# Two sets in one 64x64 stretch of TensorE, separate banks for post-mixes, scaled weights two steps ahead, and the last half tile of the value products in quadrants

## The chip, the cores and the metric

The kernel runs on one core of a Trainium2 chip. A core has TensorE (PE) for matrix products, VectorE (DVE), ScalarE (ACT) and GpSimd (POOL) for element-wise work, and SyncE (SP), whose instruction stream here issues every DMA. Each engine works through its own instructions in the order in which the program gives them, and waits on semaphores for the others. Matrix products are written to PSUM, eight banks of 128 partitions by 512 floats, and are copied from there by ScalarE or VectorE. The metric is the device time of one execution in microseconds (us), the median of several runs.

## What is computed

Eight batches of attention with 12 heads over 448 positions of 64 elements, in which the heads are mixed twice, before the softmax and after it; then a gated network without an activation function.

```python
scores = scale * np.matmul(q, k.transpose(0, 1, 3, 2))
scores = np.einsum('bhij,hg->bgij', scores, w_pre)
scores = scores - np.max(scores, axis=-1, keepdims=True)
attn = np.exp(scores)
attn = attn / (np.sum(attn, axis=-1, keepdims=True) + 1e-09)
attn = np.einsum('bhij,hg->bgij', attn, w_post)
attn_out = np.matmul(attn, v)
x = attn_out.transpose(0, 2, 1, 3).reshape(B * S, H * D)
a = x @ w1
b = x @ w2
h = a * b @ w3
return h @ w_out
```

q, k, v are 8x12x448x64, the mixing matrices 12x12, x is 3584x768, w1 and w2 768x1024, w3 1024x1024, w_out 1024x768.

## The kernel before

**Attention.** A score unit (`qk`, L173 to L187) multiplies two heads' queries and keys for a slice of 64 to 128 rows: four matmuls of 64x64 tiles into two PSUM banks, two ScalarE copies out (L178, L179), and a store to a scratch tensor in HBM (`raw_d`). The rows of scores are then read back in another order (`fetch`, L201): five rows of all 12 heads stand on 60 partitions, and four such halves make a set, two blocks (c) of ten rows. 45 blocks a batch and 8 batches make 180 sets.

Each set m goes through these methods: `mix` multiplies its four 60x448 pieces by the mixing matrix (L219, the sign turned and the scale folded in) into two banks, psm; `largest` takes minima of the negated scores on VectorE (L226); `exp` makes exponentials and their sums on ScalarE (L234); `scale` makes the reciprocals on VectorE (L243, L244) and multiplies the second mixing matrix by them on GpSimd (L246), the scaled weights; `post` multiplies the exponentials by these (L259), 28 small matmuls in the program, into banks 4 and 5, pso, which also transposes the result to keys on partitions; `put` (L273) copies both banks to `mt` on ScalarE. All of these matmuls use TensorE as 64x64 tiles.

When 15 blocks of a batch are there (a third of its rows, called a below), `av` (L300) multiplies them by the values: for each pair of heads, four tiles of keys with 128 keys each, the two heads in the two halves of the array's columns (128x64 tiles). 448 keys are three and a half tiles. The last tile holds the last 64 keys twice, and the half of `mt` that does not belong to a row's half set s is zero, kept zero by a memset of parts of pso at the start. The result of three pairs leaves one bank at once: for the first two batches as a high and a low part (L321, L322), for the others as a copy (L307) that is stored to `x_d`.

**Experts.** The network uses each operand as a high and a low part (128x128 tiles and three products for one). For the first two batches it is computed directly (L521, L552), for the other six in pairs of batches with seven products in place of eight (L701). The low parts are made on GpSimd (L640), the sums of products on VectorE (L655) and ScalarE (L657). Weights come by DMA into buffers, asked for as earlier ones are used up (L392). Before that, in the first 50 steps, w3 and w_out, given as 64-bit words, are converted (`to_f32`, four VectorE instructions a piece, L116 to L120) and multiplied into one matrix (L359); later w1 and w2 are converted as well.

**Order.** The whole order is written out by hand in `run`, as steps n, two for each set. Each engine gets its instructions in just this order. `fetch` of set m+2 stands at even steps, ahead of all other DMAs of that step. At an even step n = 2m VectorE takes the minima of set m, a share of the expert matmuls is issued (`advance`), then come the exponentials of set m, and the rest of the share. At an odd step the division and the scaled weights of set m come first, then half of the share and the other half, then value products (`avs`), the post-mix of set m-1, the pre-mix of set m+1, and score units (`qks`). So each odd step has one stretch of 64x64 work, with full-array work around it. `shares` gives each step so many expert matmuls that all steps are about equally long, with the cost of score units, value products and the rest of a stretch given in numbers of expert matmuls. Lists keep work for later: `ends` (copies out of a bank, flushed at fixed points or when a bank is needed), `soon` (the next step's start) and `later` (mainly DMAs, issued at the next step's start behind `fetch`).

PSUM banks: score units use 0 and 1 (a second one 6 and 7), pre-mixes 2 and 3, post-mixes 4 and 5, value products 0, experts 6 and 7.

## Time and profile before

| | us |
|---|---|
| median of 3 runs | 1456.61 |
| lowest and highest run | 1449.06 and 1458.63 |
| the profiled execution, its own time | 1456.61 |
| its span, from the first to the last instruction | 1454.8 |
| ScalarE's exponentials (L234), busy | 226.6 |
| GpSimd's scaled weights (L246), busy | 180.7 |
| post-mix matmuls (L259), busy | 198.6 |
| value product matmuls (L300), busy | 156.9 |

The page gives for each engine the time in which it had an instruction running. Matmuls overlap, so the sum of their durations says little; what one costs is read from the distance between starts. The program's matmuls on plain floats appear as two instructions each in the trace: the 28 of a post-mix are 56. A row "A x n" in the timeline merges n instructions of one line that follow each other. In rows of groups, the part behind the bar is busy time and mean duration, then how long the engine had been idle just before, and what ended that idle time. In the rows of waits, the numbers are the total, the count and the longest.

### The profile page before, as it was taken

How to read it: one execution, taken by the hardware profiler on the slowest of the kernel's cores; microseconds unless marked ns; L12 is line 12 of the kernel's file. 1: busy time of each engine (PE TensorE's matmuls, PEld its weight loads, DVE VectorE, ACT ScalarE, POOL GpSimd, SP SyncE). 2: the span in 40 equal slices, each digit the busy share in tenths (PEclk: the TensorE clock that was granted, in tenths of full speed). 3: DMA queues.
4: the chain of work that ended last, by engine and by line, in shares of the span. 5: the costliest groups of instructions: out<-in, count | busy, mean ns of one | idle time of the engine just before them, and what ended most of it. 6: DMA issues, size and time to landing. Idle time of an engine off the chain costs nothing.

```text
span 1454.8 us, 45722 instructions
## 1 busy us (share of the span) xinstructions
PE 1390.1 (96%) x18684; PEld 1059.4 (73%) x18684; DVE 739.0 (51%) x1497; ACT 833.1 (57%) x1952; POOL 620.7 (43%) x754
## 2 busy tenths in 40 slices
PE   5789998999999989999999999999999999999998
PEld 2357785776677667776777777777776777899988
DVE  4867565767644544432344445334444447334563
ACT  3876665777756656665555656656655546422231
POOL 1333232444324434632244445444335446446683
PEclk7989998999999999999999999999999999999999
DMA  8998789999999999999989988799879766698875
GB/s 256 365 319 274 237 267 287 311 336 307 316 288 353 348 343 319 368 338 314 311 266 291 319 278 280 234 312 350 288 230 285 236 179 214 206 332 263 240 229 173
DMA packets 203760, 416.86 MB, mean 287 GB/s; under 512 B 20528, under 2 KB 120112, under 8 KB 203472
## 3 DMA queue, kind: packets, MB, share of 16 engines
q1 hardware_dynamic: 203552, 413.94, 87.2%
q8 instruction: 149, 2.44, 0.7%
q14 instruction: 59, 0.48, 0.1%
HBM read 279.77 MB, written 134.09 MB: 284 GB/s over the span
## 4 chain that ended last, share of the span: by engine, by line
PE 78%; DMA 13%; DVE 5%; ACT 3%; issue 1%; SPq 0%; POOL 0%; DVEq 0%; ACTq 0%; POOLq 0%
PE e L701 20%; PE psa L300 10%; PE pso L259 10%; PE psm L219 8%; PE psq L173 7%; PE psf L359 5%; PE eg L521 4%; PE e2o L701 4%; PE e1o L701 4%; PE e3o L701 4%; DMA s_d<-s 3%; PE eo L552 3%; DMA cs<-wo 3%; DMA r<-raw_d 2%; DMA wu<-w_d 2%; ACT e L234 1%
## 5 line engine op out<-in xcount | busy, mean ns | idle before, releaser
L246 POOL TENSOR_SCALAR w<-wpo,ri 128x60 f32<-128x60 f32 x360 | 180.7, 518 | 489.0 <-DVE ri L244 465.8
L226 DVE TENSOR_REDUCE mn<-psm 128x1 f32<-128x448 f32 x360 | 207.8, 619 | 317.0 <-PE psm L219 316.6
L701 PE MATMUL e<-eh,wu 128*128 128x448 f32 x1008 | 297.3, 372 | 6.3 <-DVE c L655 3.2
L273 ACT COPY mt<-pso 128x480 f32<-128x480 f32 x352 | 197.8, 621 | 177.3 <-PE pso L259 177.1
L234 ACT ACTIVATE e<-psm,mn 128x448 f32<-128x448 f32 x360 | 226.6, 642 | 9.6 <-DVE mn L226 9.6
L219 PE MATMUL psm<-r,wsc 60*64 60x448 f32 (+1 forms) x1440 | 197.9, 557 | 32.1 <-ACT e L234 19.9
L701 PEld LDWEIGHTS e<-eh,wu 128*128 128x128 f32 x1008 | 188.0, 188 | 52.5 <-issue 27.4
L259 PEld LDWEIGHTS pso<-w,e 60*64 60x64 f32 x10080 | 174.5, 134 | 50.0 <-issue 44.0
L259 PE MATMUL pso<-w,e 60*64 60x60 f32 x10080 | 198.6, 224 | 0.1
L701 PE MATMUL e<-el,wu 128*128 128x448 f32 x504 | 187.1, 371 | 0.0
L173 PE MATMUL psq<-kq 64*64 64x448 f32 x1176 | 159.5, 546 | 0.6 <-ACT st L178 0.6
L300 PE MATMUL psa<-mt,v 128*64 128x150 f32 (+1 forms) x2304 | 156.9, 293 | 1.9 <-ACT st L178 1.9
L300 PEld LDWEIGHTS psa<-mt,v 128*64 128x64 f32 x2304 | 143.6, 137 | 17.9 <-issue 6.3
L655 DVE TENSOR_TENSOR c<-c,e 128x448 f32<-128x448 f32 x168 | 101.8, 618 | 87.6 <-PE e L701 82.8
L178 ACT COPY st<-psq 128x448 f32<-128x448 f32 x162 | 86.4, 533 | 68.8 <-ACT mt L273 32.8
L521 PE MATMUL eg<-xh,wu 128*128 128x448 f32 x384 | 118.8, 380 | 4.8 <-DMA wu<-w_d 4.8
L640 POOL TENSOR_TENSOR el<-x,eh 128x448 fp32r<-128x448 f32 x90 | 104.2, 1176 | 34.8 <-ACT eh L639 34.8
L701 PEld LDWEIGHTS e<-el,wu 128*128 128x128 f32 x504 | 94.9, 188 | 22.4 <-issue 14.1
L243 DVE TENSOR_SCALAR sa<-sm 128x2 f32<-128x2 f32 x180 | 35.9, 200 | 129.6 <-ACT e L234 129.0
L173 PEld LDWEIGHTS psq<-kq 64*64 64x64 f32 x1176 | 62.2, 136 | 53.8 <-issue 29.8
L521 PEld LDWEIGHTS eg<-xh,wu 128*128 128x128 f32 x384 | 71.8, 190 | 38.1 <-issue 25.3
L179 ACT COPY st<-psq 128x448 f32<-128x448 f32 x162 | 87.7, 541 | 0.0
(99 smaller groups left out, 2011.5 us busy)
## 6 DMA issues: line engine op xcount, KB each, us to landing
r<-raw_d SPq DMA_DIRECT2D x344, 210.0 KB, 4.9
raw_d<-st SPq DMA_DIRECT2D x138, 448.0 KB, 5.4
wu<-w_d SPq DMA_DIRECT2D x104, 384.0 KB, 6.4
wu<-s_d SPq DMA_DIRECT2D x96, 384.0 KB, 4.8
wu<-w_d SPq DMA_DIRECT2D x51, 512.0 KB, 5.6
kq<-kq SPq DMA_DIRECT2D x42, 448.0 KB, 6.2
wu<-s_d SPq DMA_DIRECT2D x36, 512.0 KB, 4.9
x<-x_d SPq DMA_DIRECT2D x72, 224.0 KB, 6.3
```

The source lines that it names most:

```text
L173: nc.tensor.matmul(ps[s][z * PP:(z + 1) * PP], t[rows, q:q + PP], t[rows, k:k + S], start=True, stop=True)
L219: nc.tensor.matmul(ps[s][c * PP:(c + 1) * PP, :S], self.wsc[k], r[k, c], start=True, stop=True)
L226: self.nc.vector.tensor_reduce(mn[:, s:s + 1], self.psm[m][s][:, :S], axis=AX.X, op=ALU.min)
L234: nc.scalar.activation(e, p[:, :S], AF.Exp, bias=mn[:, s:s + 1], scale=-1.0, accum_out=sm[:, s:s + 1])
L246: nc.gpsimd.tensor_scalar_mul(w2[:, s], self.wpo, ri[:, s:s + 1])
L259: nc.tensor.matmul(self.pso[c][z * PP:(z + 1) * PP, at:at + HK], e[k, j * PP:(j + 1) * PP], w2s[k, s], start=True, stop=True)
L273: self.nc.scalar.copy(dst.rearrange("p j g (s i) -> p j s g i", s=2), src)
L300: nc.tensor.matmul(self.psa[rows, g % 3, :W], v[:, j, rows], mt[:, j, 2 * g + s, :W], start=(j == 0), stop=(j == NJ - 1))
L521: nc.tensor.matmul(p, u[:, k % (K1 // 2), x], xs[y][:, k], start=(k == 0 and t == 0), stop=(k == K1 - 1 and t == 2))
L640: nc.gpsimd.tensor_tensor(lo, x, hi.bitcast(F32), op=ALU.subtract)
L655: nc.vector.tensor_tensor(a[out], a[to[0]], p, op=ALU.add)
L701: nc.tensor.matmul(p, w[:, k, x], ops[m, k][y], start=(k == 0 and t == 0), stop=(k == nk - 1 and t == 2))
```

## The change

Steps are grouped by four, for two sets m and m+1 (m even). Step 0 of a group: fetch of both next sets, minima and exponentials of m and m+1. Step 1: divisions and scaled weights of both. Step 3: value products, then post-mix of m, a score unit, post-mix of m+1, pre-mix of m+2, a score unit, pre-mix of m+3, one stretch of 64x64 work. Expert matmuls go to steps 0 to 2. Conversions go on in all steps; at step 3 they come behind the stretch.

The pre-mix and the post-mix of even sets use banks 4 and 5, those of odd sets banks 0 and 1. Score units use banks 2 and 3. One of the two copies of a post-mix is made by VectorE. In `mt` a third's rows are now ordered by half set, then block (s, u, i).

A call of `av` now does two head pairs, in three calls for each third instead of two. The first three key tiles go as before into bank 1; of the last half tile, each half set's columns (75, or 73 at the end of a batch) are multiplied by the 64 keys on their own partitions, into bank 0 for one half set and another part of bank 1 for the other, as four 64x64 tiles. A copy on ScalarE and additions on VectorE join the two and restore the order of rows (`join`). For the first two batches, the high part is then a ScalarE copy and the low part a GpSimd subtraction. In most places the value products come ahead of the post-mix in step 3; for four of the 24 thirds they stand in the steps 0 to 2.

```diff
     def mix(self, m):
-        ps = [self.bank(2 + s, f"psm{m}_{s}") for s in range(2)]
+        ps = [self.bank((4, 0)[m % 2] + s, f"psm{m}_{s}") for s in range(2)]
...
     def post(self, m):
         nc, w2s = self.nc, self.w2s.pop(m)
-        if any(b in (4, 5) for b, _ in self.ends):
-            self.do_ends()
+        ps = [self.bank((4, 0)[m % 2] + c, f"pso{m}_{c}") for c in range(2)]
...
-            dst = self.mt[b, a][:, :, :, u * IB:u * IB + w]
-            self.ends.append((4 + c, lambda dst=dst, src=src, w=w: self.put(dst, src, w)))
+            dst = self.mt[b, a].rearrange("p j g (s i) -> p j s g i", s=2)[:, :, :, :, u * IH:(u + 1) * IH]
+            copy, w = nc.vector.tensor_copy if c else nc.scalar.copy, self.width(2 * m + c)
+            self.ends.append(((4, 0)[m % 2] + c, lambda copy=copy, dst=dst, src=src, w=w: self.put(copy, dst, src, w)))
...
-    def av(self, b, a, g):
...
-        for j in range(NJ):
-            for s in range(2):
-                rows = slice(s * D, (s + 1) * D)
-                nc.tensor.matmul(self.psa[rows, g % 3, :W], v[:, j, rows], mt[:, j, 2 * g + s, :W],
-                                 start=(j == 0), stop=(j == NJ - 1))
...
+    def av(self, b, a, half):
+        nc, cols, mt = self.nc, self.cols(a), self.mt[b, a]
+        W, us, Q = cols.stop - cols.start, (2 * half, 2 * half + 1), GB * IH
+        ends, wide = (Q, W), self.bank(1, f"psa{b}_{a}_{half}")
+        ps = wide[:, :2 * GB * IB].rearrange("p (g i) -> p g i", g=2)
+        tail = [x.rearrange("p (g i) -> p g i", g=2) for x in (self.bank(0, f"psb{b}_{a}_{half}")[:, :2 * Q], wide[:, 4 * Q:6 * Q])]
+        for g, u in enumerate(us):
+            for j in range(NJ - 1):
+                for s in range(2):
+                    rows = slice(s * D, (s + 1) * D)
+                    nc.tensor.matmul(ps[rows, g, :W], self.vs[b, u][:, j, rows], mt[:, j, 2 * u + s, :W],
+                                     start=(j == 0), stop=(j == NJ - 2))
+        for g, u in enumerate(us):
+            for t in range(2):
+                k, w = slice(t * PP, (t + 1) * PP), slice(t * Q, ends[t])
+                for s in range(2):
+                    rows = slice(s * D, (s + 1) * D)
+                    nc.tensor.matmul(tail[t][rows, g, :w.stop - w.start], self.vs[b, u][k, NJ - 1, rows], mt[k, NJ - 1, 2 * u + s, w],
+                                     start=True, stop=True)
...
+        def join():
+            if W == GB * IB:
+                nc.scalar.copy(x.rearrange("p g (u s i) -> p g s u i", s=2, i=IH), ps.rearrange("p g (s u i) -> p g s u i", s=2, i=IH))
+            else:
+                for y, p, _ in pieces():
+                    nc.scalar.copy(y, p)
+            for y, _, q in pieces():
+                nc.vector.tensor_tensor(y, y, q, op=ALU.add)
...
+            nc.scalar.copy(h, x[:, :, :W])
+            nc.gpsimd.tensor_tensor(l, x[:, :, :W], h.bitcast(F32), op=ALU.subtract)
...
+        early = [0, 1, 2, 3, 3, 4, 5, 6, 7, 7, 8, 9, 10, 11, 11]
...
+                n = 13 + i // 3 * 4 + (i % 3 > 0) * 2 if b == 1 else 43 + ((b - 2) * 21 + i) * NB // 84 * 4
...
+        for k in range(B * NG):
+            b, a = divmod(k, NG)
+            done = ((k + 1) * GB - 1) // 4 * 4 + 4
+            for half in range(HP // 2):
+                avs.setdefault(done + half if k + 1 in (3, 12, 18, 24) else done + 3 + 4 * half, []).append((b, a, half))
...
-            other = [len(qks.get(n, [])) * 3.7 + len(avs.get(n, [])) * 5.1 + n % 2 * 9.3 for n in range(first, last)]
+            other = [len(qks.get(n, [])) * (3.7 if n % 4 == 3 else 5.3) + len(avs.get(n, [])) * 10 + (n % 4 == 3) * 16.2
+                     for n in range(first, last)]
...
-            m, odd = divmod(n, 2)
-            if not odd and LF <= n + LF < N:
-                self.fetch(m + LF // 2)
+            m, at = n // 4 * 2, n % 4
+            if at == 0:
+                for x in (m + 2, m + 3):
+                    if x < SETS:
+                        self.fetch(x)
             self.do_later()
...
+            if at == 0:
+                for x in sets:
+                    self.largest(x)
+            if at < 3:
+                convert()
             advance(now // 2)
             self.do_ends()
-            if not odd and m < SETS:
-                self.exp(m)
+            for x in sets:
+                if at == 0:
+                    self.exp(x)
+                elif at == 1:
+                    self.scale(x)
             advance(now - now // 2)
             for x in avs.get(n, []):
                 self.av(*x)
+                self.do_ends()
...
+            if at == 3 and m < SETS:
+                for x in (m, m + 1):
+                    self.post(x)
+                    self.do_ends()
+                    if x == m:
+                        scores()
+                for x in (m + 2, m + 3):
+                    if x < SETS:
+                        self.mix(x)
+                        if x == m + 2:
+                            scores()
+            while units:
+                scores()
             self.do_ends()
...
+            if at == 3:
+                self.do_soon()
+                convert()
```

`convert` holds what ran a conversion's piece before, and the sums of weights for the seven products.

130 lines of the change are left out of this document (57 added, 73 removed).

## The prediction, made before the changed kernel was run

> **What bounds the kernel now.** I read the page first, then busy time by stage, then TensorE's timeline in a steady stretch, then the waits.
>
> ```profile
> span 1454.8 us, 45722 instructions
> PE 1390.1 (96%) x18684; PEld 1059.4 (73%) x18684; DVE 739.0 (51%) x1497; ACT 833.1 (57%) x1952; POOL 620.7 (43%) x754
> ...
> q1 hardware_dynamic: 203552, 413.94, 87.2%
> ...
> PE 78%; DMA 13%; DVE 5%; ACT 3%; issue 1%; SPq 0%; POOL 0%; DVEq 0%; ACTq 0%; POOLq 0%
> ```
>
> TensorE is the bound (96% busy, 78% of the chain), and the DMA engines are close behind (87% over the whole span). Busy time by stage, columns as PE, PEld, DVE, ACT, POOL, granted clock, DMA share, GB/s:
>
> ```profile
> 0.00:100.00 100.00, 68.37 (x789) 33.51 (x791) 69.21 (x138) 64.11 (x149) 30.87 (x43) 0.86 0.96 324
> 100.00:240.00 140.00, 136.77 (x2027) 106.77 (x2027) 86.82 (x182) 89.64 (x216) 39.90 (x58) 1.00 0.82 260
> 240.00:400.00 160.00, 151.58 (x2361) 106.48 (x2361) 108.44 (x229) 118.44 (x283) 64.60 (x88) 0.97 0.95 314
> 400.00:700.00 300.00, 289.00 (x4387) 212.46 (x4388) 127.66 (x274) 185.80 (x441) 118.25 (x146) 0.99 0.99 335
> 700.00:1270.00 570.00, 564.79 (x8190) 436.91 (x8189) 255.35 (x547) 329.95 (x777) 256.68 (x328) 1.00 0.84 266
> 580.00:600.00 20.00, 20.00 (x273) 14.57 (x274) 11.46 (x24) 14.66 (x35) 14.08 (x15) 1.00 1.02 379
> ```
>
> The limits differ. Before 100 us TensorE idles a third of the time. From 240 to 400 us VectorE and ScalarE are 68% and 74% busy. From 400 to 700 us DMA stands at 0.99, though 20 us of it moved 379 GB/s against the mean of 335. From 700 us on nothing but TensorE is near its limit, so time taken off TensorE there is time gained. By 1270 us attention has ended and the change has nothing to touch. Now what TensorE's busy time holds:
>
> ```profile
> 702.34 0.37 PE L701 MATMUL e<-eh,wu 128*128 128x448 f32 x1
> 702.63 1.08 PE L259 MATMUL pso<-w,e 60*64 60x60 f32 x55
> 703.49 0.54 PE L219 MATMUL psm<-r,wsc 60*64 60x448 f32 x1
> 703.50 0.22 PE L259 MATMUL pso<-w,e 60*64 60x60 f32 x1
> 703.50 0.98 PE L219 MATMUL psm<-r,wsc 60*64 60x448 f32 x7
> 704.25 0.98 PE L173 MATMUL psq<-kq 64*64 64x448 f32 x8
> 705.16 0.47 PE L701 MATMUL e<-eh,wu 128*128 128x448 f32 x1
> 705.47 0.36 PE L701 MATMUL e<-el,wu 128*128 128x448 f32 x1
> 705.67 0.57 PE L701 MATMUL e<-eh,wu 128*128 128x448 f32 x2
> 706.08 0.37 PE L701 MATMUL e<-el,wu 128*128 128x448 f32 x1
> ...
> 708.40 3.28 PE L300 MATMUL psa<-mt,v 128*64 128x150 f32 x48
> 711.61 1.08 PE L259 MATMUL pso<-w,e 60*64 60x60 f32 x55
> ```
>
> Read start to start. Expert matmuls of the full array come every 0.20 us (705.47 to 705.67; two in 0.41 after that). The last one before the 64x64 stretch holds 0.29 us until post-mix starts: 0.09 too much. In the stretch, post-mix takes 0.87 us (56 instructions, 15.5 ns each), pre-mix 0.75 us for 8, and nothing is lost between them. The score unit takes 0.91 instead of the same 0.75 until the experts resume (0.16 too much), and the first expert matmul then holds 0.31 instead of 0.20 (0.11). Entering and leaving a 64x64 stretch thus costs 0.09 + 0.16 + 0.11 = 0.36, say 0.35 us, all counted as busy. The value products take 3.21 us for 48, 66.9 ns each.
>
> **Fewer stretches.** Before, each of 180 sets has its own stretch, and 17 steps hold score units alone: 197 (counted from the schedule). After, 90 stretches hold two sets each, and 28 steps hold score units or value products alone: 118. That removes 79 x 0.35 = 27.7 us of TensorE.
>
> **Value products.** Each batch, block and head pair needs 16 instructions, 4 key tiles of 4. The last tile is half zeros. After, 12 full-height instructions stay, and 8 of 75 columns run as four 64x64 quadrants. No row has these. Bounds: 15.5 ns each (post-mix's pitch at 60 columns) and 19.4 ns (the same by columns, 15.5 x 75/60). Pre-mix's 94 ns for 448 columns gives 15.7 by columns, so I take the middle, 17.5 ns. Per head pair 4 x 66.9 = 268 ns become 8 x 17.5 = 140; 144 of them save 18.4 us (bounds 16 to 20.7). Gross gain 27.7 + 18.4 = 46 us, 0.256 per set.
>
> The Trainium skill (TensorE: Matmul & The Clock Gate, Part 1, "Wait — 56ns, not 53.3ns?") says that starts of matmuls never come closer than about 25 ns. By that rule the quads would take 8 x 25 = 200 ns and save only 9.7 us. The trace speaks against it for quadrants: post-mix starts 56 instructions in 0.87 us.
>
> **What goes to other engines.**
>
> ```profile
> L226 DVE TENSOR_REDUCE mn<-psm 128x1 f32<-128x448 f32 x360 | 207.8, 619 | 317.0 <-PE psm L219 316.6
> L273 ACT COPY mt<-pso 128x480 f32<-128x480 f32 x352 | 197.8, 621 | 177.3 <-PE pso L259 177.1
> L219 PE MATMUL psm<-r,wsc 60*64 60x448 f32 (+1 forms) x1440 | 197.9, 557 | 32.1 <-ACT e L234 19.9
> L655 DVE TENSOR_TENSOR c<-c,e 128x448 f32<-128x448 f32 x168 | 101.8, 618 | 87.6 <-PE e L701 82.8
> L243 DVE TENSOR_SCALAR sa<-sm 128x2 f32<-128x2 f32 x180 | 35.9, 200 | 129.6 <-ACT e L234 129.0
> ...
> 700.74 0.64 ACT L234 ACTIVATE e<-psm,mn 128x448 f32<-128x448 f32 x1
> 701.36 0.64 ACT L234 ACTIVATE e<-psm,mn 128x448 f32<-128x448 f32 x1
> 703.76 1.12 ACT L273 COPY mt<-pso 128x480 f32<-128x480 f32 x2 [0.32 <-PE pso L259]
> 705.30 0.53 ACT L178 COPY st<-psq 128x448 f32<-128x448 f32 x1 [0.42 <-ACT mt L273]
> 705.73 0.54 ACT L179 COPY st<-psq 128x448 f32<-128x448 f32 x1
> ...
> 718.73 3.32 POOL L640 TENSOR_TENSOR el<-t,eh 128x448 fp32r<-128x448 f32 x3
> 702.72 1.05 POOL L246 TENSOR_SCALAR w<-wpo,ri 128x60 f32<-128x60 f32 x2 [1.12 <-DVE ri L244]
> SPq L201 <- PE psm L219: 310.4, 110, 6.4
> ```
>
> One post-mix copy of each set moves to VectorE: 180 x 0.62 = 112 us off ScalarE. On VectorE no row copies 480 strided elements; 448 elements cost 0.62 in L655 and L226, so 0.62 to 0.66. The joins add 144 VectorE adds of 150 elements, between L243's 0.20 and L655's 0.62; by elements 0.34, together 49 us, and 72 ScalarE copies in place of 36. The two first batches' low parts go to GpSimd. VectorE rises to about 900 us, 63%, which is no bound over the span, but in 100 to 400 us it is close: 25 sets (1400 post-mix instructions at 56) lie in 240 to 400, and 25 x (0.62 + 0.27) = 22 us on top of 108 makes 130 of some 154.
>
> Within the long stretch: post-mix ends at 0.87, first score unit at 1.62, second post-mix at 2.49, pre-mix at 3.24, second score unit at 3.99, pre-mix at 4.74. ScalarE's post-mix copy runs 1.1 to 1.7, the two score copies 1.9 to 2.9 (0.43 apart), the other set's copy 2.9 to 3.5, so banks 2 and 3 are free at 2.9 for the second score unit (3.24), and banks 0 and 1 at 3.5 for the last pre-mix (3.99). VectorE's two adds (0.68) end some 1.4 us after the value products, before 1.62. It fits when both engines come in idle; for late ones I take 0.05 us a stretch, 4 us.
>
> The chain to the next stretch, from this one's start: minima of the second set end at 6.1, ScalarE's four exponentials (one per 0.62, 700.74 to 701.36) begin behind the last score copies at 5.2 and end at 7.7; the division (0.4 a set) stands in VectorE's queue behind the expert sums of step two, then four scaled weights on GpSimd at 0.42 to 0.52 end near 10.5 to 12. From 700 us on the next post-mix comes at 12.3 (35 expert matmuls in three steps) or 2 us later with value products ahead of it, and its second set 1.6 later. Slack is 0.5 to 3 us; the old order had 8 (the weights begun at 702.72 served the post-mix of 711.61). GpSimd's low-part subtractions (1.1 us each, three in 3.32) can stand ahead. I take 0.05 us mean, 2 us over 41 stretches.
>
> The moved score units bring the same two ScalarE copies and one store each; with banks 2 and 3 alone, the second waits for the first's copies, with a pre-mix queued behind it on TensorE (above: 0.3 us to spare). The value products now also wait for what the odd set left in banks 0 and 1: exponentials that ended two steps earlier, and in four places, where the products stand in the same step as them, perhaps 2 us each, which is inside the 4 us. The first batch's score units are pulled forward by three steps into time that the conversions set. Stores of the value products become 54 instead of 36 with the same bytes.
>
> Loads of two sets are asked together; SP then stands at them until the second pre-mix, as it stands 310 us at L201 now, with score stores, weight and value loads queued behind. Bytes stay the same. From 400 to 700 us it decides how evenly the DMA engines are fed, and 3.8% more speed needs 348 GB/s: I keep half of that stage's gain. Weights of the experts are asked one step apart, four ahead in three steps: no cost.
>
> **The sum**, in sets by stage (post-mix counts 448, 1064, 1400, 2520, 4648, at 56 a set): 8, 19, 25, 45 and 83, worth 2.0, 4.9, 6.4, 11.5 and 21.2 us. Given back: the first 240 us all (6.9; conversions and DMA set the pace), 240 to 400 half (3.2), 400 to 700 half (5.7), in-stretch 4, chain 2. Returned: of the 19.9 us in which pre-mix waits for exponentials (L219), 3 us, since the shared bank is now asked for three steps later. 46 - 6.9 - 3.2 - 5.7 - 6 + 3 = 27. The profiled execution took 1456.6 us (span 1454.8 and 1.8 around it), which is the median of the runs, so 1429.5.
>
> **Rivals.** (1) Everything kept: 1456.6 - 46 = 1410. For it: 99% busy from 700 us on; against: 0.99 DMA share before. Chance 0.15. (2) VectorE's queue binds before 400 us: conversions stand ahead of minima and division, and each of 22 stretches there loses 1 us, while 400 to 700 keeps nothing: 1429.5 + 22 + 6 = 1457, no change. The 85% load worked out above speaks for it; chance 0.20. (3) Slower: scaled weights arrive late in steady state. If three subtractions stand ahead of them in half of the 90 stretches and each then loses 1.1 us, that is +50: 1479. Break-even is a mean loss of 27/90 = 0.30 us a stretch. Against it: the weights' 1.05 us pair is small beside the two steps left. Chance 0.10. (4) The quads start no faster than 25 ns: 18.4 - 9.7 = 8.7 less, 1438. The page named above has that rule; post-mix's 15.5 ns rules against it. Chance 0.05.
>
> **How the numbers follow.** The forecast has 0.50, with its own range of 1417 to 1443. The range runs from 1406 (just under rival 1) to 1463, which takes in rival 2. Faster by over 1% (below 1442; about what a measurement of this kernel can tell): 0.45 of the forecast, all of rival 1 and 0.04 of rival 4: 0.64. Within 1%: 0.05 + 0.18 + 0.01 = 0.24. Slower: 0.12.
>
> **What would show it.** Right: about 118 entries into 64x64, each still costing 0.35; quads at 15.5 to 19.4 ns; TensorE's busy time down by some 45 us; almost no idle before post-mix after 700 us. Wrong: post-mix waiting on the scaled weights or on VectorE's adds (rival 3), TensorE idle below 400 us up by 20 us (rival 2), DMA waits of hundreds of ns a step from 400 to 700 us.

## The result, and the profile after

The changed kernel takes 1526.4 us in the median of 4 runs (1525.4 to 1529.8), the kernel before 1457.6 beside it: a ratio of 1.048, with an interval from 1.044 to 1.052. It is 4.8% slower, where 1.9% faster was forecast. The profiled execution took 1527.1 us. Lines of its page:

```profile
span 1525.3 us, 47548 instructions
PE 1390.4 (91%) x19260; PEld 1091.4 (72%) x19260; DVE 897.2 (59%) x1861; ACT 760.5 (50%) x1882; POOL 632.0 (41%) x772
...
q1 hardware_dynamic: 203840, 413.94, 83.0%
...
PE 67%; DMA 13%; DVE 7%; ACT 5%; issue 4%; POOL 2%; SPq 1%; DVEq 0%; ACTq 0%; POOLq 0%
```

The span grew by 70.5 us. TensorE's busy time is the same as before (1390.4 against 1390.1), so all 70 us are idle time of TensorE (134.9 against 64.7). VectorE (897) and ScalarE (760) carry what was forecast; neither is full over the span. DMA is less busy than before, for the same bytes.

**Where the time went.** To compare nearly the same work, the span is cut where VectorE starts the division (L243) of sets 60, 90 and 178. Busy time by stage of the kernel before (columns as in the prediction: PE, PEld, DVE, ACT, POOL, granted clock, DMA share, GB/s):

```profile
0.00:445.60 445.60, 402.32 (x5869) 281.32 (x5870) 284.64 (x590) 300.97 (x714) 150.75 (x208) 0.96 0.91 298
445.60:646.10 200.50, 193.06 (x2923) 141.75 (x2922) 93.17 (x198) 127.55 (x304) 92.87 (x108) 0.99 1.00 344
646.10:1257.00 610.90, 602.13 (x8743) 462.33 (x8741) 264.90 (x571) 353.42 (x832) 257.24 (x336) 1.00 0.85 273
```

And of the changed kernel:

```profile
0.00:487.80 487.80, 408.91 (x6102) 297.09 (x6103) 321.91 (x696) 283.45 (x701) 161.71 (x226) 0.92 0.84 272
487.80:722.00 234.20, 202.40 (x3063) 154.31 (x3061) 127.75 (x263) 114.88 (x293) 85.45 (x108) 0.92 0.91 306
722.00:1329.00 607.00, 588.58 (x8955) 468.10 (x8955) 348.15 (x753) 313.47 (x787) 268.80 (x340) 1.00 0.83 271
```

| sets | time | TensorE idle | TensorE busy | forecast gross gain, at 0.256 a set | clock missing while TensorE is busy, before and after |
|---|---|---|---|---|---|
| 0 to 60 | +42.2 | +35.6 | +6.6 | 15.4 | 13.1 and 30.9 |
| 60 to 90 | +33.7 | +24.4 | +9.3 | 7.7 | 1.7 and 15.8 |
| 90 to 178 | -3.9 | +9.6 | -13.5 | 22.5 | 1.7 and 2.0 |

The last column adds up, from the trace's record of the granted clock, half of the time in which TensorE was busy while half the clock was granted. (One minus the mean clock of a stage, times its length, gives more, 17.8 and 39.0 in the first stage, because it also counts a low clock while TensorE stands idle.) In the first two stages the missing clock grew by 17.8 and 14.1 us. This is more than the 15.4 and 7.7 us that the forecast takes off, so busy time rose there. So the loss has two parts: TensorE waits longer (60 us up to set 90), and after waiting it runs slower (32 us). From set 90 on the clock is full and there is a gain, but of 4 us, not of some 20.

**What TensorE waits for.** Groups of TensorE's instructions, before and then after; behind the bar are busy time, mean ns, and the idle time just before them with what ended it:

```profile
L259 PE MATMUL pso<-w,e 60*64 60x60 f32 x10080 | 198.6, 224 | 0.1
L219 PE MATMUL psm<-r,wsc 60*64 60x448 f32 (+1 forms) x1440 | 197.9, 557 | 32.1 <-ACT e L234 19.9 <-DMA r<-raw_d 11.1 <-ACT eh L639 1.0
L300 PE MATMUL psa<-mt,v 128*64 128x150 f32 (+1 forms) x2304 | 156.9, 293 | 1.9 <-ACT st L178 1.9
L521 PE MATMUL eg<-xh,wu 128*128 128x448 f32 x384 | 118.8, 380 | 4.8 <-DMA wu<-w_d 4.8
```

```profile
L258 PE MATMUL bank<-w,e 60*64 60x60 f32 x10080 | 208.5, 227 | 54.5 <-POOL w L246 26.2 <-DVE xd L328 18.8 <-issue 8.3
L219 PE MATMUL bank<-r,wsc 60*64 60x448 f32 (+1 forms) x1440 | 205.8, 572 | 24.9 <-DMA r<-raw_d 9.6 <-ACT mt L272 8.7 <-issue 4.6
L300 PE MATMUL bank<-mt,v 128*64 128x150 f32 (+1 forms) x1728 | 127.8, 298 | 13.1 <-ACT e L234 9.3 <-DVE xd L328 3.5 <-ACT eh2o L663 0.3
L545 PE MATMUL eg<-xh,wu 128*128 128x448 f32 x384 | 118.4, 380 | 11.6 <-DMA wu<-w_d 11.5
```

Post-mix never waited before (0.1 us in 180 sets) and now waits 54.5 us, for the scaled weights (L246) and for VectorE's additions in the joins (L328, which free banks 0 and 1 for the odd set). Value products wait 11 us more, the weights of the experts 7 more, pre-mix 7 less. Together that is 65 of the 70 us.

**An undisturbed stretch.** TensorE's timeline late in attention, with value products in front:

```profile
906.26 0.37 PE L725 MATMUL e<-el,wu 128*128 128x448 f32 x1
906.55 1.73 PE L300 MATMUL bank<-mt,v 128*64 128x148 f32 x24
908.22 0.48 PE L307 MATMUL bank<-mt,v 64*64 64x75 f32 x16
908.53 1.03 PE L258 MATMUL bank<-w,e 60*64 60x60 f32 x55
...
909.35 0.97 PE L173 MATMUL psq<-kq 64*64 64x448 f32 x7
910.10 1.03 PE L258 MATMUL bank<-w,e 60*64 60x60 f32 x55
...
910.92 0.97 PE L219 MATMUL bank<-r,wsc 60*64 60x448 f32 x7
911.67 0.98 PE L173 MATMUL psq<-kq 64*64 64x448 f32 x8
912.42 0.98 PE L219 MATMUL bank<-r,wsc 60*64 60x448 f32 x8
913.33 0.67 PE L725 MATMUL e<-eh,wu 128*128 128x448 f32 x2
```

But for the value products it runs as the prediction has it, start to start: 16 quadrant instructions in 0.31 us (19.4 ns each), a post-mix in 0.82, a score unit or pre-mix in 0.75, and the same loss when it is entered (0.29 in place of 0.20) and left (0.91 in place of 0.75). The 24 full-height value products take 1.67 us, 69.6 ns each, where the prediction has 66.9. Counted in the trace, TensorE leaves the full-array matmuls 106 times in place of 184.

**A stretch that waits, case C.** The timeline of all engines around 270 us, cut to the rows that make the chain:

```profile
263.58 0.35 DVE L116 TENSOR_SCALAR ca<-cs 128x384 int32<-128x384 int32 x1
...
264.21 0.98 PE L219 MATMUL bank<-r,wsc 60*64 60x448 f32 x8
...
265.97 0.56 DVE L120 SCALAR_TENSOR_TENSOR cx<-cm,ca 128x384 f32<-128x384 f32 x1 [0.85 <-ACT cm L106]
266.44 2.21 DVE L226 TENSOR_REDUCE mn<-bank 128x1 f32<-128x448 f32 x4
...
268.57 0.35 DVE L116 TENSOR_SCALAR ca<-cs 128x384 int32<-128x384 int32 x1
...
270.62 0.56 DVE L120 SCALAR_TENSOR_TENSOR cx<-cm,ca 128x384 f32<-128x384 f32 x1 [0.51 <-ACT cm L106]
271.10 0.16 DVE L243 TENSOR_SCALAR sa<-sm 128x2 f32<-128x2 f32 x1
...
271.65 2.21 POOL L246 TENSOR_SCALAR w<-wpo,ri 128x60 f32<-128x60 f32 x4 [4.25 <-DVE sa L243]
272.33 1.81 PE L258 MATMUL bank<-w,e 60*64 60x60 f32 x56 [2.64 <-POOL w L246]
273.87 1.77 PE L173 MATMUL psq<-kq 64*64 64x448 f32 x8
```

Both pre-mixes are done by 265.2, yet VectorE first finishes a conversion (263.58 to 266.5, with a wait for ScalarE's `cm`), then takes four minima, then does a second conversion, which waits for ScalarE again, and only then the division, at 271.10. GpSimd has been idle for 4.25 us, TensorE for 2.64. And the post-mix that follows takes 1.54 us from start to start (272.33 to 273.87) instead of 0.82. The clock in the windows around it says why:

```profile
270.00:272.30 2.30, 0.00 (x0) 0.00 (x0) 1.68 (x8) 1.87 (x5) 0.65 (x2) 0.96 1.04 395
272.30:274.00 1.70, 1.67 (x60) 1.68 (x64) 0.83 (x2) 0.00 (x0) 1.70 (x4) 0.50 0.92 296
274.00:276.00 2.00, 2.00 (x52) 1.09 (x49) 1.15 (x1) 0.95 (x2) 1.77 (x2) 0.62 0.62 226
276.00:278.00 2.00, 2.00 (x48) 1.30 (x41) 1.42 (x4) 1.16 (x3) 0.00 (x0) 1.00 0.95 244
```

Half the clock is granted for 1.7 us, and 0.62 of it in the mean of the next 2 (half until 275.5, then all of it): another 1.70 x 0.50 + 2.00 x 0.38 = 1.6 us lost after a wait of 2.64. The Trainium skill (TensorE: Matmul & The Clock Gate, Part 1, "What's actually happening") says that the gate falls back to half speed after an idle window of about 3.4 us. The trace agrees in the half speed, and shows it after a shorter wait.

**Case J.** The timeline again, 13 us later. A join's additions stand behind a conversion:

```profile
287.82 1.33 DVE L120 SCALAR_TENSOR_TENSOR cx<-cm,ca 128x384 f32<-128x384 f32 x1 [1.70 <-POOL wu L126]
...
289.07 0.52 DVE L328 TENSOR_TENSOR xd<-xd,bank 128x150 f32<-128x150 f32 x2
...
289.52 1.16 PE L258 MATMUL bank<-w,e 60*64 60x60 f32 x51 [2.02 <-DVE xd L328]
```

The conversion waits 1.70 us for a buffer that GpSimd frees, the additions wait behind it, and the odd set's post-mix waits 2.02 us for the bank.

**Case D.** The timeline near 600 us, where experts' weights are being summed. Each piece of a sum is stored by DMA, and the engine that writes the next piece waits at the head of its queue until a buffer is free:

```profile
594.83 0.81 SPq L509 DMA_DIRECT2D s_d<-s  x2
...
601.01 0.51 ACT L506 CAST s<-y 128x384 fp32r<-128x384 f32 x1 [10.42 <-DMA s_d<-s]
...
601.89 0.61 ACT L272 COPY mt<-bank 128x480 f32<-128x480 f32 x1
...
602.56 1.38 PE L219 MATMUL bank<-r,wsc 60*64 60x448 f32 x8 [3.89 <-ACT mt L272]
```

ScalarE waits 10.42 us for a buffer, until a store (`s_d<-s`) out of it has run; the copy out of a post-mix bank stands behind that cast, and the pre-mix, 3.89 us late, behind the copy. On SP these stores stand behind `fetch`, where SP now waits 332.5 us in all and up to 10.6 at once (310.4 and 6.4 before). In the case shown SP spent the time on issuing: it began four loads of `fetch` at 584.20, loads of values at 588.33, two kinds of stores after them, and only at 594.83 these two stores, whose second halves GpSimd (L507) had written by 589.2.

### The profile page after: what moved, and what is told of

Same layout as the page of the kernel before. It is cut to its first block, busy times and chain, and to the rows that moved or that the text cites. A ratio compares the mean times of both kernels' runs of the same rounds, so it can differ in the third digit from the quotient of the medians.

```text
span 1525.3 us, 47548 instructions
## 1 busy us (share of the span) xinstructions
PE 1390.4 (91%) x19260; PEld 1091.4 (72%) x19260; DVE 897.2 (59%) x1861; ACT 760.5 (50%) x1882; POOL 632.0 (41%) x772
## 4 chain that ended last, share of the span: by engine, by line
PE 67%; DMA 13%; DVE 7%; ACT 5%; issue 4%; POOL 2%; SPq 1%; DVEq 0%; ACTq 0%; POOLq 0%
PE e L725 18%; PE bank L258 8%; PE bank L219 8%; PE psq L173 7%; PE bank L300 7%; PE e3o L725 3%; PE e2o L725 3%; PE psf L383 3%; PE eo L576 3%; DMA raw_d<-st 2%; ACT e L234 2%; PE e1o L725 2%; DMA r<-raw_d 2%; PE eg L545 2%; DMA x<-x_d 2%
## 5 line engine op out<-in xcount | busy, mean ns | idle before, releaser
L258 PEld LDWEIGHTS bank<-w,e 60*64 60x64 f32 x10080 | 204.3, 141 | 98.2 <-POOL w L246 37.8
L246 POOL TENSOR_SCALAR w<-wpo,ri 128x60 f32<-128x60 f32 x360 | 175.2, 508 | 200.7 <-DVE sa L243 163.6
L258 PE MATMUL bank<-w,e 60*64 60x60 f32 x10080 | 208.5, 227 | 54.5 <-POOL w L246 26.2
L234 ACT ACTIVATE e<-bank,mn 128x448 f32<-128x448 f32 x360 | 224.0, 642 | 36.3 <-DVE mn L226 36.3
L226 DVE TENSOR_REDUCE mn<-bank 128x1 f32<-128x448 f32 x360 | 203.9, 616 | 48.4 <-PE bank L219 41.1
L219 PE MATMUL bank<-r,wsc 60*64 60x448 f32 (+1 forms) x1440 | 205.8, 572 | 24.9 <-DMA r<-raw_d 9.6
L272 DVE COPY mt<-bank 128x480 f32<-128x480 f32 x176 | 115.0, 655 | 133.6 <-PE bank L258 133.6
L272 ACT COPY mt<-bank 128x480 f32<-128x480 f32 x176 | 110.5, 628 | 115.8 <-PE bank L258 115.5
L328 DVE TENSOR_TENSOR xd<-xd,bank 128x150 f32<-128x150 f32 (+1 forms) x192 | 41.6, 267 | 175.9 <-ACT xd L323 119.9
L300 PE MATMUL bank<-mt,v 128*64 128x150 f32 (+1 forms) x1728 | 127.8, 298 | 13.1 <-ACT e L234 9.3
L178 ACT COPY st<-psq 128x448 f32<-128x448 f32 x162 | 86.4, 533 | 105.3 <-PE psq L173 52.9
L300 PEld LDWEIGHTS bank<-mt,v 128*64 128x64 f32 x1728 | 107.4, 138 | 35.8 <-issue 15.0
```

Of the source, the lines that this page charges most:

```text
L219: nc.tensor.matmul(ps[s][c * PP:(c + 1) * PP, :S], self.wsc[k], r[k, c], start=True, stop=True)
L226: self.nc.vector.tensor_reduce(mn[:, s:s + 1], self.psm[m][s][:, :S], axis=AX.X, op=ALU.min)
L234: nc.scalar.activation(e, p[:, :S], AF.Exp, bias=mn[:, s:s + 1], scale=-1.0, accum_out=sm[:, s:s + 1])
L246: nc.gpsimd.tensor_scalar_mul(w2[:, s], self.wpo, ri[:, s:s + 1])
L258: nc.tensor.matmul(ps[c][z * PP:(z + 1) * PP, at:at + HK], e[k, j * PP:(j + 1) * PP], w2s[k, s], start=True, stop=True)
L272: copy(dst, src)
```

## The experiments

The theories named in the expectations: C, VectorE's queue puts conversions ahead of minima, division and joins; J, the joins hold the odd set's post-mix; D, ScalarE, VectorE and SP stand at transfers that come late, with the chain of the sets queued behind. All ratios are to the kernel before on the same chip, with a 95% interval. Differences to the changed kernel are differences of these ratios in points of a per cent; a point is 14.6 us. Most ratios are good to 0.3 or 0.4 points (e2's to 0.6, e10's to 0.5), so a difference of half a point (e1, e5, e6, e10) is at the edge of what can be told. Figures by sets come from one execution each: those of e12 and e15 differ by 7 us up to set 60, with medians 0.6 us apart, so a few us by sets say little. All results:

| run | median us | ratio (interval) | points against the change |
|---|---|---|---|
| the change | 1526.4 | 1.0481 (1.0444 to 1.0517) | |
| e1 chain of the sets first in VectorE's queue | 1518.2 | 1.0435 (1.0405 to 1.0465) | -0.46 |
| e2 half of the conversion left out | 1507.9 | 1.0385 (1.0324 to 1.0447) | -0.96 |
| e4 joins' additions left out | 1504.3 | 1.0361 (1.0325 to 1.0397) | -1.20 |
| e5 post-mix with unscaled weights | 1515.2 | 1.0430 (1.0402 to 1.0458) | -0.51 |
| e6 a fourth buffer for pieces | 1515.9 | 1.0431 (1.0393 to 1.0470) | -0.50 |
| e11 fetch behind the other DMAs | 1506.1 | 1.0329 (1.0284 to 1.0374) | -1.52 |
| e9 = e2 + e4 + e5 + e6 | 1481.9 | 1.0172 (1.0128 to 1.0217) | -3.09 |
| e13 = e9 + e11 | 1459.8 | 1.0054 (1.0029 to 1.0079) | -4.27 |
| e14 = e1 + e6 + e11 | 1503.9 | 1.0349 (1.0318 to 1.0380) | -1.32 |
| e8 odd post-mix behind the even set's pre-mix | 1564.3 | 1.0767 (1.0735 to 1.0799) | +2.86 |
| e10 both post-mix copies on ScalarE | 1536.2 | 1.0528 (1.0474 to 1.0581) | +0.47 |
| e16 every second score copy on VectorE | 1557.4 | 1.0730 (1.0688 to 1.0772) | +2.49 |
| e3 old order, quadrants only | 1458.1 | 1.0017 (0.9993 to 1.0041) | |
| e7 kernel before, half of the conversion left out | 1450.8 | 0.9991 (0.9970 to 1.0012) | |
| e12 old order, quadrants for batches 4 to 7 | 1451.1 | 0.9962 (0.9935 to 0.9988) | |
| e15 = e12 with fetch behind the other DMAs | 1450.6 | 0.9978 (0.9954 to 1.0002) | |

**e1.** The minima of the next group are issued right behind the stretch, the division ahead of the conversion.

```diff
-            if at == 0:
+            if n == 0:
                 for x in sets:
                     self.largest(x)
+            if at == 1:
+                for x in sets:
+                    self.scale(x)
...
             if at == 3:
+                for x in (m + 2, m + 3):
+                    if x < SETS:
+                        self.largest(x)
                 self.do_soon()
```

> The changed kernel (1526 us) with the minima of the next two sets put right behind the long stretch, ahead of the conversion, and divisions and scaled weights put at the start of step 1, ahead of the conversion there. Theory C (VectorE's queue has conversions ahead of minima and division): the idle before post-mix that ends with the scaled weights (26 us on TensorE) goes to under 8, and the time falls to 1495 or less. Theory J (the joins of the value products on VectorE hold the odd set's post-mix): 1520 or more, since the joins are now later, not earlier. Theory D (heads of ScalarE's and VectorE's queues that wait for DMAs): within 6 us of 1526.

Post-mix's idle time fell only from 54.5 to 47.2 us:

```profile
L258 PE MATMUL bank<-w,e 60*64 60x60 f32 x10080 | 203.6, 224 | 47.2 <-DVE xd L328 24.0 <-POOL w L246 16.3 <-issue 5.7
```

Waits for the scaled weights went from 26.2 to 16.3, where C named under 8, and the time is between what C and J named; waits for the joins rose from 18.8 to 24.0. C is true in part. It would fit that the conversion still goes ahead of something, now of the joins, but this is argued and not shown.

**e2 and e7.** Two of a conversion's four VectorE instructions are left out, so the converted weights lack their sign and lowest bits: in the changed kernel (e2), and as a control in the kernel before (e7).

```diff
-        nc.vector.scalar_tensor_tensor(a, top, -0x40000000, a, op0=ALU.bitwise_and, op1=ALU.bitwise_or)
-        nc.vector.scalar_tensor_tensor(a, low, 29, a, op0=ALU.logical_shift_right, op1=ALU.bitwise_or)
```

> The changed kernel with two of the four VectorE instructions of each conversion left out (72 pieces, 1.2 us each, so the weights are wrong values). Theory C: most of what was lost in the first 400 us (38 us against the kernel before, by the times of the sets) comes back, 1495 or less. Theories J and D: about 1515, only the load taken off at the start, where TensorE waits for conversions in both kernels.

> The kernel before with the same two VectorE instructions of each conversion left out: the control for the same cut in the changed kernel, which gave 18 us. If the load of conversions is what the change suffers from, this gives less than 6 us (1448 or more). If it gives 12 or more, the cut says nothing about the change.

The changed kernel gains 0.96 points, the kernel before 0.09, within its interval. So VectorE's load of conversions costs time in the new order alone, some 13 us for half of it. The size is rough: the four runs of e2 lie between 1502 and 1523 us, and 1508 stands between the 1495 of C and the 1515 of the other theories.

**e3.** The quadrants by themselves: the change's `av` and its order of rows in `mt`, with everything else in the old order. The lines are shown against the changed kernel.

```diff
-        ps = [self.bank((4, 0)[m % 2] + s, f"psm{m}_{s}") for s in range(2)]
+        ps = [self.bank(2 + s, f"psm{m}_{s}") for s in range(2)]
...
-            for half in range(HP // 2):
-                avs.setdefault(done + half if k + 1 in (3, 12, 18, 24) else done + 3 + 4 * half, []).append((b, a, half))
+                for half in range(HP // 2):
+                    n = (b * NB + (a + 1) * GB + 3) | 1
+                    avs.setdefault(n + (2 - (a == NG - 1)) * half, []).append((b, a, half))
```

> The kernel before with the value products of the change (two head pairs a call, last half tile in quadrants, join on ScalarE and VectorE) and nothing else of it: one set a stretch, score units, banks of post-mixes and order as before. The prediction's term alone: 18 us less and some 3 us for eight more stretches, 1440 to 1446. Theory J: the join itself costs, since score units use the same banks 0 and 1 behind it: 1460 or more.

```profile
PE 1378.7 (95%) x19260; PEld 1046.4 (72%) x19260; DVE 775.9 (53%) x1677; ACT 850.9 (59%) x2066; POOL 633.8 (44%) x772
```

TensorE's busy time falls by 11.4 us, and the time does not move: 72.8 us of the 1451.5 of this span are idle, 64.7 before. The value products themselves, added up from start to start in the trace, hold TensorE for 144.6 us in place of 153.5: some 9 us are saved, not 18.4. By sets, the time from set 90 to 178 falls by 9.9 us and the rest takes 7 of that back.

**e4.** The additions of the joins are left out, so the last half tile is missing from the result.

```diff
-            for y, _, q in pieces():
-                nc.vector.tensor_tensor(y, y, q, op=ALU.add)
```

> The changed kernel without the 192 VectorE additions of the join, so that the last 64 keys are left out of the result; the quadrant matmuls still run. Theory J: the idle that ends with the joins (22 us) goes, with the lower clock behind it, 1500 or less. Theory C: 1515, as the scaled weights stay late. Theory D: 1515 to 1526.

```profile
L258 PE MATMUL bank<-w,e 60*64 60x60 f32 x10080 | 200.3, 225 | 33.1 <-POOL w L246 15.3 <-ACT cm L106 9.3 <-issue 4.0
```

Additions that take VectorE 42 us (L328, 192 at 267 ns), on an engine that is 59% busy, cost 1.20 points, 17 us, at 1504 against the 1500 that J named. J is shown; and with the additions the wait for the scaled weights falls too, since they stand in one queue.

**e5.** `post` multiplies by the plain mixing matrix; the scaled weights are still made, but nobody waits for them, so the softmax is not normalized.

```diff
-                    nc.tensor.matmul(ps[c][z * PP:(z + 1) * PP, at:at + HK], e[k, j * PP:(j + 1) * PP], w2s[k, s],
+                    nc.tensor.matmul(ps[c][z * PP:(z + 1) * PP, at:at + HK], e[k, j * PP:(j + 1) * PP], self.wpo[k],
...
```

> The changed kernel with post-mixes that use the second mixing matrix itself, so that the division is left out of the result; reciprocals and scaled weights are still made, but nothing waits for them. Theory C in its wide form (the path from pre-mix over minima, exponentials, division and scaled weights is too long for three short steps): the first 8 sets lose at most 10 us against before instead of 19.5, sets 32 to 90 at most 30 instead of 52, 1490 or less. Theory D (heads of queues that wait for DMAs): 1515 or more. Theory J: 1510.

The wait for L246 (26.2 us) is gone by construction and 0.51 points are gained, 7 us: the wide form of C, which named 1490, is not borne out. Of the rest, part reappears at the joins (21.8 us in place of 18.8) and at pre-mix (35.2 in place of 24.9).

**e6.** A fourth buffer for the pieces of conversions and sums.

```diff
-        s = self.cs.tile([128, CW, 2], I32, tag="s", name=f"cs{name}", bufs=3)
+        s = self.cs.tile([128, CW, 2], I32, tag="s", name=f"cs{name}", bufs=4)
...
-            s = self.cs.tile([128, CW, 2], I32, tag="s", name=f"s{w}_{f}_{m}", bufs=3)
+            s = self.cs.tile([128, CW, 2], I32, tag="s", name=f"s{w}_{f}_{m}", bufs=4)
```

> The changed kernel with four instead of three staging buffers for 64-bit words and for split sums of weights (3 KB more a partition). Theory D: ScalarE's casts of sums no longer wait for their stores (28 us of ScalarE idle), sets 60 to 90 lose 15 us less, 1510 or less. Theories C and J: within 6 us of 1526.

A gain of 0.50 points; the 1510 that D named was not reached. By sets, 60 to 90 lose 21.2 us instead of 33.7, the others nothing less, so the gain lies where case D does.

**e8.** The odd set's post-mix is put behind the even set's next pre-mix, which gives its weights and the joins 0.75 us more.

```diff
                     self.do_ends()
-                    if x == m:
-                        scores()
-                for x in (m + 2, m + 3):
-                    if x < SETS:
-                        self.mix(x)
-                        if x == m + 2:
-                            scores()
+                    scores()
+                    if x + 2 < SETS:
+                        self.mix(x + 2)
```

> The changed kernel with the stretch in the order post-mix, score unit, pre-mix of the even set, then the same of the odd set, nothing left out: the odd set's post-mix starts 0.75 us later and the even set's pre-mix 0.75 us earlier. Theories C and J: each wait before the odd post-mix shrinks by 0.75 us, some 20 of them, with the clock behind them: 1500 to 1512. Theory D: within 6 us of 1526.

Weight loads of the pre-mix that wait for the post-mix copies, in the waits of the changed kernel and then of e8:

```profile
PEld bank L219 <- ACT mt L272: 29.9, 58, 4.0
```

```profile
PEld bank L219 <- ACT mt L272: 136.9, 170, 6.1
```

No theory had this: all three named a time near the change's or below it. Each pre-mix now stands at most one score unit behind the post-mix of its own two banks, and waits for the copies out of them (170 times, 58 in the change). The relief for post-mix (27 us of idle time before it instead of 54.5) is paid back more than once.

**e9 and e13.** The edits of e2, e4, e5 and e6 in one kernel, and then e11's with them; what those leave out is left out here too.

> The changed kernel with four cuts at once: half of the conversions' VectorE instructions, the join's additions and the division in the post-mix left out of the computation, and four staging buffers. Alone they gave 18, 22, 11 and 10 us. If each is a cause of its own, the sum holds: 1526 - 61 = 1465. If the waits stand in for one another (one goes and the next one binds), the gain is larger together, and the time falls under 1450, towards the forecast of 1429. If something else holds the stretch (copies out of the banks, the lower clock, loads), more than 1475.

> The four cuts of the earlier run (1482 us; half of the conversions' VectorE work, the join's additions and the division in the post-mix left out of the computation, four staging buffers) together with the loads of the next sets asked last (20 us alone). If the order on SP is a cause of its own: 1460 to 1466. If it and the cuts remove the same waits: 1475 or more. If this removes the last of the waits: 1445 or less.

The four single gains add up to 3.17 points, together they give 3.09; with e11's 1.52 that makes 4.61, and e13 gives 4.27. Within the intervals they add. (The 1465 that e9's expectation named for a plain sum was added up in us from runs on different chips; by the ratios, each to the kernel before on its own chip, the sum is 46 us and not 61. The branch above 1475, that something else holds the stretch too, is borne out by e11.) Post-mix and the last long stage in e13, from its groups and its windows:

```profile
L255 PE MATMUL bank<-wpo,e 60*64 60x60 f32 x10080 | 197.1, 222 | 9.7 <-issue 7.1 <-ACT e L232 2.1 <-ACT xd L323 0.3
```

```profile
0.00:454.88 454.88, 404.17 (x6102) 290.88 (x6103) 228.20 (x497) 281.51 (x701) 154.69 (x226) 0.94 0.91 293
454.88:656.94 202.06, 188.99 (x3020) 143.72 (x3019) 121.50 (x228) 114.32 (x287) 83.89 (x108) 0.97 0.97 343
656.94:1260.77 603.83, 589.48 (x8998) 470.47 (x8999) 331.66 (x663) 315.42 (x795) 268.69 (x340) 1.00 0.86 276
```

With the five causes out, post-mix waits 9.7 us, and the loss of 76 us up to set 90 is down to 11 (454.9 + 202.1 against 646.1). But the kernel is still 0.5% slower than the one before (0.3 to 0.8), not faster: 9 of those 11 lie before set 60, and sets 90 to 178 gain 7 us and no more.

**e10.** Both copies of a post-mix on ScalarE again.

```diff
-            copy, w = nc.vector.tensor_copy if c else nc.scalar.copy, self.width(2 * m + c)
+            copy, w = nc.scalar.copy, self.width(2 * m + c)
```

> The changed kernel with both copies of a post-mix on ScalarE, as before the change, nothing left out. If it is VectorE's queue in the stretch that hurts (theory C and J): 1500 to 1515, as pre-mixes no longer wait for it and its load falls by 115 us. If ScalarE's copies are the tighter side (30 us of weight loads wait for them now): 1535 or more.

No better, rather worse, with intervals that overlap; 1536 is at the edge of what was named for ScalarE's copies as the tighter side. Post-mix's idle time stays at 53.6 us: 100 us of copies taken off VectorE (897 to 797) and put on ScalarE do not shorten the wait.

**e11.** `fetch` is issued behind the DMAs that are kept for later and the loads of queries and keys.

```diff
-            if at == 0:
-                for x in (m + 2, m + 3):
-                    if x < SETS:
-                        self.fetch(x)
             self.do_later()
...
                 self.load_kq(*x)
+            if at == 0:
+                for x in (m + 2, m + 3):
+                    if x < SETS:
+                        self.fetch(x)
```

> The changed kernel with the loads of both next sets asked behind the stores and the loads of weights, values and queries of step 0 instead of ahead of them. Theory D in the form that SP stands at these loads with everything else behind it: waits for expert weights (12 us on TensorE) fall under 6, sets 60 to 90 lose 8 us less, 1512 or less. Otherwise within 6 us of 1526, or slower where pre-mix waits for its rows.

The largest single gain, 1.52 points or 22 us, with four lines moved. SP's waits at `fetch` (L201) for a pre-mix to have read its buffers fall from 332.5 us to 26.3. The stage of sets 60 to 90, and then a row of the waits, in e11:

```profile
485.00:695.54 210.54, 193.06 (x3063) 148.41 (x3061) 130.83 (x263) 115.73 (x294) 85.67 (x108) 0.97 0.97 339
```

```profile
ACT s L506 <- DMA s_d<-s: 13.3, 6, 4.6
```

The stage takes 210.5 us instead of 234.2, with DMA at 339 GB/s instead of 306 and the clock at 0.97 instead of 0.92. The wait of case D was at most 10.4 us and is at most 4.6. D is shown, and its place on SP: the loads of two sets stand at its head, in part until the last pre-mix has read their buffers, and everything else is issued behind them.

**e12 and e15.** The quadrants only where TensorE is the bound, for batches 4 to 7, in the old order; e15 has e11's move as well.

```diff
-                self.av(*x)
+                (self.av_old if x[0] < QUADS else self.av)(*x)
```

These lines are the dispatch alone, against the kernel before; `QUADS` is 4 and `av_old` is the method of the kernel before.

> The kernel before with the change's value products for batches 4 to 7 alone, and the old ones for the rest, nothing left out. With quads everywhere in the old order, sets 90 to 180 gained 10 us and the sets ahead of them lost 5. If that reading by stage holds: 8 to 10 us under the kernel before, 1444. If not (the run-to-run spread of stages): within 4 us of it.

> The kernel before with the change's value products for batches 4 to 7 (1451 us, 0.9962 of before) and its loads of sets asked behind the stores and other loads of the step. If the place of these loads on SP matters in the old order too: 5 us less, 1446. If it matters only where two sets are asked at once: within 3 us of 1451, or slower.

e12 is 0.4% faster than the kernel before (0.9935 to 0.9988), the only version whose interval lies below the kernel before. Its 5.5 us are fewer than 9, half of the forecast for the quadrants, and near half of the 9 us that e3's value products saved. SP's order makes no difference there (e15), though SP's waits at `fetch` fall as in e11, from 312.3 us to 32.1; why nothing was lost behind them in the old order is not shown.

**e14.** The three repairs that leave the result whole, e1 + e6 + e11.

> The changed kernel with three mends, nothing left out: minima and division ahead of conversions (8 us alone), four staging buffers (10) and loads of sets asked last (20). Added up 1526 - 38 = 1488; with overlap of the last two, which both act between sets 60 and 90, 1495. Still slower than before in either case. Below 1460 would mean that the order on the queues is the whole loss.

It is no better than e11 alone, and slower than the 1488 to 1495 expected. By sets (0 to 60, 60 to 90, 90 to 178) it loses 32.6, 15.2 and 0.1 us to the kernel before, e11 39.4, 10.0 and 0.4. So some of e1's gain before set 60 may be there and something is lost after it, but these are differences at the edge, and why the gains of e1 and e6 vanish was not settled. The grouped order was not made to pay.

**e16.** The second copy of every score unit on VectorE.

```diff
-        (nc.vector.tensor_copy if b == c == 0 else nc.scalar.copy)(st[:, 1], ps[1])
+        nc.vector.tensor_copy(st[:, 1], ps[1])
```

> The changed kernel with one of the two copies of each score unit on VectorE, nothing left out. If hesitations within the stretch come from ScalarE having four of its six copies (pre-mix's weights wait 30 us for ScalarE's post-mix copy): sets 90 to 178 lose 8 us less, 1515 or less. If VectorE's queue is the later one: 1530 or more, with sets before 60 losing more.

2.5 points slower. Post-mix waits 63.2 us, and value products 26.3 instead of 13.1, mostly for exponentials, whose minima come later on VectorE. Neither queue had room: work put on ScalarE's (e10) gained nothing, work put on VectorE's cost 2.5 points, though in the change VectorE was busy for 59% of the span.

## Why the prediction was wrong

**Right: what TensorE itself does.** The loss at entering and leaving a stretch, the pitches of post-mix, pre-mix and score unit, the number of stretches saved (78, forecast 79), and nearly the pitch of the quadrants (19.4 ns, which is the upper bound given; 17.5 was taken). The rule about 25 ns, rival 4, is contradicted. VectorE's and ScalarE's totals came as forecast, VectorE's strided copy too (655 ns for 0.62 to 0.66). Pre-mix's waits fell by 7 us where 3 were taken.

**Wrong: the size of the value products' term.** It had 18.4 us; e3 shows 9. The 66.9 ns of a full-height instruction is a mean over a call of 48 in which the last one, before the smaller tiles, holds TensorE for 220 ns and each other one for 63.4 (start to start in the trace). So an instruction left out saves 63.4 (2 us less in all); this hand-over happens in 72 calls and no longer in 48, which was counted at nothing (4 us); and the quadrants with what follows them take 20.8 ns each in e3 (4 us). The size is what rival 4 would have taken off, for another reason.

**Wrong, and by far the larger part: the terms of what is given back.** The sum had 16 us given back before 700 us, as a share of the gain and never more than the gain itself, and 6 for late chains. Measured by sets, sets 0 to 90 lost 76 us against the kernel before, where the sum had 23 of gross gain.

1. *"Conversions and DMA set the pace" up to 240 us, "half" to 400.* This capped the loss at zero. The forecast looked at VectorE's load (85%) and left the queue's order to rival 2, at 1 us a stretch for 22 stretches. What counted was what stands in front of the sets' chain (e2, e4, in part e1), not VectorE's total (e10), and case C cost 2.6 us of waiting and 1.6 of clock in one stretch.
2. *The chain, "0.05 us mean, 2 us".* It was worked out for the stage from 700 us on, where nothing else stands in VectorE's queue, and there it held: the waits of sets 90 to 178 have 3.9 us before post-mix, 1.1 of them for the scaled weights. Before set 90 it did not. The old order had 8 us of slack for the chain, and post-mix waited 0.1 us; the new one has 0.5 to 3, by the prediction's own working, and post-mix waits 54.5. The number was on the page and was not applied to the stages in which conversions fill the gap.
3. *The joins, "two adds (0.68) end before 1.62".* Right when VectorE comes in idle (the two took 0.52), wrong behind a conversion. They cost 17 us (e4).
4. *"Fetch ... with score stores, weight and value loads queued behind", "half of that stage's gain".* The place was named and the price was one half of 11 us; e11 shows 22.
5. *The clock* was not in the sum at all. The clock missing while TensorE was busy grew by some 32 us in the first two stages (17.8 + 14.1). Every wait was priced at its length, and costs about half as much again: 32 us beside 60 of added idle time there, and 1.6 beside 2.64 in the one case shown.

Rival 2's mechanism and the "chain" of rival 3 both occurred, rival 2's with case D beside it, where the prediction had them as alternatives with one price each. Rival 3, the slower one at 1479, had the right kind of wait in the wrong place: it expected it in the steady state, and it came before set 90.

**What stays open.** From set 90 to 178 the clock is full, and still only 13.5 of 22.5 us leave TensorE's busy time (about 10 for equal work, since value products of 68 head pairs lie in that stage after and of 72 before), and 9.6 come back as idle time. The five cuts of e13 do not change that (busy 589.5 against 588.6). Added up from start to start, two terms fall short there. The value products save some 5 us for equal work, not 9. And the 88 pre-mixes hold TensorE for 79.6 us in place of 71.8, of which the exit that now stands behind a pre-mix in every stretch explains about 2.6. Pre-mix weights that wait for ScalarE's copies (L272) stand in the list of waits with 16.3 us in that stage, with 0.4 before, but a part of these waits is hidden, and no run took them away alone. Nor do the runs show why sets 0 to 60 still lose 9 us in e13, and no run has the grouped order with the old value products.

## What to carry to other kernels

Putting two small stretches together saves the entries of one, but it also lumps together what every other engine owes to it, and takes away the slack that hid those queues. Before such a change, take each engine's queue and ask what stands in front of the instruction that the next stretch needs, at the worst place and not in the steady state; a half-empty engine can still be late. Price a wait of TensorE with the slow clock behind it; and when a burst of loads goes to the head of a DMA-issuing queue, ask what is stuck behind it.

## What the runs showed of the hardware

Quadrant matmuls of 64x64 by 75 columns start 19.4 ns apart (16 in 0.31 us), and the post-mix's of 60 columns 14.5 to 15.5. The last 128x64 matmul before 64x64 tiles held TensorE for 0.22 us, the others of its call for 0.063. The granted clock was at half already after a wait of 2.64 us, and it was full again 3.2 us after the work had resumed (272.3 to 275.5).
